# A GEGLU feed-forward kernel: sixteen start-up transposes in one run, and the first two token blocks loaded in halves

## The chip, the core and the metric

The kernel runs on one core of one Trainium2 chip. The time is device time in microseconds of one execution. Three executions took 300.17, 300.36 and 300.91 us, a median of 300.36. A fourth execution, which took 300.01 us, was profiled; its span from the first to the last instruction is 298.7 us.

## What is computed

```python
B, S, D, F = 32, 32, 1024, 3584          # x is (B, S, D), all bfloat16
def reference(x, w_gate, w_up, w_down):
    return (_gelu(x @ w_gate) * (x @ w_up)) @ w_down
```

With tokens flattened there are N = 1024 tokens, D = 1024 features and F = 3584 hidden features. GELU is the tanh approximation.

## The kernel before

It is written engine by engine: each of the five engines has a program (`prog_sp`, `prog_act`, `prog_pool`, `prog_pe`, `prog_dve`, L317 to L482) whose instructions run in the order written. Order between engines is kept by counting semaphores ("clocks"): `wait` stops an engine's program until a count is reached.

**The tiling.** F is cut into 28 chunks of 128 hidden features. A "part" (L140 to L149) is one chunk against one range of tokens, and gives a gate product (key G) and an up product (key U), each the sum of eight matmuls over the eight slices dk of D. ScalarE applies GELU to the gate sum (L442), VectorE multiplies by the up sum (L475) and writes the hidden activations `hT`. After all parts, TensorE multiplies `hT` with `w_down` in 17 jobs (L423).

**x must be transposed**, since a matmul wants D on the partitions. There are two ways of doing it here.

- The first 256 tokens (`XA`) are two blocks b of 128 tokens. Each is loaded with tokens on the partitions (`xa`, L295): block 0 by SP's queue, block 1 by ACT's. TensorE turns each of the 2 x 8 squares of 128 x 128 by a matmul against an identity (`turn_xa`, L349 to L359) into PSUM banks 3 to 7, as listed in `XA_PS` (L130): bank 3 takes dk 0, bank 4 dk 1, bank 5 dk 2 and 3, bank 6 dk 4 and 5, bank 7 dk 6 and 7. Each bank is then copied to `xT` (`xa_copy`, L302 to L307): bank 7 by ScalarE, where `ACT_EARLY` = 9 places the copy behind its ninth early load, the others by VectorE.
- The other 768 tokens (pieces `XB1`, `XB2`, `XC2`) are loaded by L285 and transposed by VectorE in squares of 32 (L466). `dve_order` (L50 to L58) mixes these with VectorE's products: `E` is a product, `A`, `B`, `C`, `D` are transposes of the pieces, the digit is the part or the dk.

**The start on TensorE** (`prog_pe`, L395): 14 matmuls on constants (`WARM`: six with 512 columns, eight with 128), then a wait for the identity and for both blocks of x, then the list `steps` (L36 to L47):

```python
steps += [("X", 0), ("X", 1), ("X", 2)]    # turn banks 3, 4, 5
together(range(0, 4), 0, 1)                # parts 0-3: G then U, dk 0
steps += [("X", 3), ("X", 4)]              # turn banks 6, 7
together(range(0, 4), 1, 2)                # parts 0-3, dk 1
together(range(4, 8), 0, 2)
together(range(0, 8), 2, 6)
```

As bank 5 holds dk 2 and 3, the first line has eight transposes and the fourth line the other eight. Parts 0 to 7 sum in banks 0 to 7, so part 3's first matmul also waits until bank 3 is copied out, part 4's until bank 4 is, and so on. Parts 8 to 15 are the same chunks against tokens 256 to 511, and parts 16 to 23 the same chunks against tokens 512 to 1023.

**The first weights** are pieces `W0` (L134): for dk 0 and 1 two pieces of 128 KB each (512 columns), then 256 KB pieces. SP issues those of `w_gate`, ACT those of `w_up` (`early_loads`, L294 to L300), after the block of x and ahead of the other pieces of x. Every matmul waits for its own piece (L370).

Of the kernel before, what the change touches and what calls it, by code (L numbers as in the profile page):

```python
# [5 lines left out]
P = 128  # L6
# [49 lines left out]
class _Ctx:  # L56
# [11 lines left out]
    def set(self, key, val):  # L68
        assert key not in self.cur, key
        if self.prev is not None and key in self.prev:  # L70
            assert self.prev[key] == val, (key, self.prev[key], val)
        elif self.emit:
            raise AssertionError(f"mark {key} unknown in emit pass")
        self.cur[key] = val
        return val
# [9 lines left out]
def bass_standalone__geglu_ffn__sampling_kernel(  # L85
# [13 lines left out]
    DK = D // P  # L99
# [29 lines left out]
    XPIECES = [XB1, XB2, XC2]  # L129
    XA_PS = [(3, 0, 1), (4, 1, 2), (5, 2, 4), (6, 4, 6), (7, 6, 8)]  # L130
    XA_ACT = (4,)
    ACT_EARLY = 9

    W0 = [(0, 1, 0, 512), (1, 2, 0, 512), (0, 1, 512, 1024), (1, 2, 512, 1024)]  # L134
    W0 += [(k, k + 1, 0, 1024) for k in range(2, 6)]
# [10 lines left out]
    for n, (m, h) in enumerate(rest):  # L146
        b = 2 * (n % 4)
# [13 lines left out]
    steps = []  # L161

    def together(ps_, k0, k1, tok=None):
        for dk in range(k0, k1):
            for key in ("G", "U"):
                for p in ps_:
                    steps.append((p, key, dk, tok))
# [4 lines left out]
                for dk in range(k0, DK):  # L172
                    steps.append((p, key, dk, None))

    steps += [("X", 0), ("X", 1), ("X", 2)]
    together(range(0, 4), 0, 1)
    steps += [("X", 3), ("X", 4)]
    together(range(0, 4), 1, 2)
    together(range(4, 8), 0, 2)
    together(range(0, 8), 2, 6)  # L180
    one_by_one(range(0, 8), 6)
# [26 lines left out]
    def evac_eng_is_act(ji):  # L208
        return ji % 2 == 0

    out_r = of.rearrange("(tc p) d -> p tc d", p=P)
    xa_r = xf.rearrange("(b p) d -> p b d", p=P)
# [5 lines left out]
    C_PE = _Clock("pe")  # L218
    C_ACT = _Clock("act")
    C_DVE = _Clock("dve")  # L220
    C_POOL = _Clock("pool")
    Q_XA = [_Clock(f"xa{b}", 16) for b in range(2)]
    Q_X = {(q, s): _Clock(f"x{i}{s}", 16) for i, q in enumerate(XPIECES) for s in range(2)}
    Q_W0 = {(w, p): _Clock(f"{w}0k{p[0]}c{p[2]}", 16) for p in W0 for w in ("wg", "wu")}
    Q_WG = [_Clock(f"wg{j}", 16) for j in range(NG)]
    Q_WU = [_Clock(f"wu{j}", 16) for j in range(NG)]
    Q_WD_SP = _Clock("wd_sp", 16)
    Q_WD_POOL = _Clock("wd_pool", 16)
    Q_OUT = _Clock("out", 16)
    all_clocks = [C_PE, C_ACT, C_DVE, C_POOL, *Q_XA, *Q_X.values(), *Q_W0.values(), *Q_WG, *Q_WU,  # L230
                  Q_WD_SP, Q_WD_POOL, Q_OUT]

    ctx = _Ctx()

    with ExitStack() as es:
        def sb(name, shape, dtype):
            return es.enter_context(nc.sbuf_tensor(name, shape, dtype))
# [6 lines left out]
        xa = hT[:, FM - 10:FM - 8, :]  # L244
        ident = sb("ident", [P, P], BF16)
# [8 lines left out]
        ps = es.enter_context(nc.psum_tensor("ps", [P, 8, 512], FP32))  # L254
# [27 lines left out]
        def load_x(ew, eng, q, side):  # L282
            c0, c1 = q[0] // 32, q[1] // 32
            for a in (2 * side, 2 * side + 1):
                v = ew.do(lambda: eng.dma_start(  # L285
                    xs[32 * a:32 * (a + 1), c0:c1, :], x_r[a, :, c0:c1, :]), clock=Q_X[(q, side)])
            ctx.set(("x", q, side), v)

        def load_w0(ew, eng, w, p):
            k0, k1, f0, f1 = p  # L290
            ctx.set((w + "0", p), ew.do(lambda: eng.dma_start(
                big[w][:, k0:k1, f0:f1], w_r[w][:, k0:k1, f0:f1]), clock=Q_W0[(w, p)]))

        def early_loads(ew, eng, side):  # L294
            yield ctx.set(("xa", side), ew.do(lambda: eng.dma_start(  # L295
                xa[:, side, :], xa_r[:, side, :]), clock=Q_XA[side]))
            for p in W0:
                yield load_w0(ew, eng, ("wg", "wu")[side], p)
            for q in XPIECES:
                yield load_x(ew, eng, q, side)  # L300
# [45 lines left out]
                    osb[:, tc, col0:col0 + ncols]), clock=Q_OUT)  # L346
            sp.wait(Q_OUT, last)

        def turn_xa(pe, eng, j):  # L349
            bank, k0, k1 = XA_PS[j]  # L350
            for dk in range(k0, k1):
                for b in range(2):
                    o = 256 * (dk - k0) + P * b
                    last = dk == k1 - 1 and b == 1
                    v = pe.do(lambda: eng.matmul(  # L355
                        ps[:, bank, o:o + P],
                        xa[:, b, :].rearrange("p (j k) -> p j k", k=DK)[:, :, dk],
                        ident[:, :], start=(dk == k0 and b == 0), stop=last), mark=last)
            ctx.set(("XP", j), v)  # L359

        def part_step(pe, eng, opened, i, key, dk, tok):
            m, t0, t1, gs, us = parts[i]
            w, (bank, f0, f1) = ("wg", gs) if key == "G" else ("wu", us)
            if tok is not None:
                f0, f1 = f0 + tok[0] - t0, f0 + tok[1] - t0
                t0, t1 = tok
            buf, slot, j = slot_of[m]
            if j is None:
                p = next(p for p in W0 if p[0] <= dk < p[1] and p[2] <= m * P < p[3])
                pe.wait(Q_W0[(w, p)], ctx.get((w + "0", p)))  # L370
            else:
                pe.wait((Q_WG if w == "wg" else Q_WU)[j], ctx.get((w, j)))
            if bank in bank_before[i]:
                pe.wait(C_DVE, ctx.get(("D", bank_before[i][bank])))
            for jx, (xbank, k0, k1) in enumerate(XA_PS):
                if t0 == XA[0] and (xbank == bank or k0 <= dk < k1):
                    pe.wait(C_ACT if jx in XA_ACT else C_DVE, ctx.get(("XA", jx)))
            for q in XPIECES:
                if q[0] < t1 and t0 < q[1]:
                    pe.wait(C_DVE, ctx.get(("T", dk, q)))  # L380
            first = (i, bank) not in opened
            opened.add((i, bank))
            last = (dk == DK - 1)
            v = pe.do(lambda: eng.matmul(  # L384
                ps[:, bank, f0:f1],
                wbuf(w, buf)[:, dk, slot * P:(slot + 1) * P],
                xT[:, dk, t0:t1],
                start=first, stop=last and (key == "U" or gs[0] != us[0]),
            ), mark=last)
            if last:  # L390
                ctx.set((key, i), v)

        WARM = [512] * 6 + [128] * 8

        def prog_pe(eng):  # L395
            pe = _Eng(ctx, eng, C_PE)
            for n in WARM:
                pe.do(lambda: eng.matmul(ps[:, 0, 0:n], ones_w, ones_x[:, 0:n],  # L398
                                         start=True, stop=True), mark=False)
            pe.wait(C_POOL, ctx.get("ident"))  # L400
            for b in range(2):
                pe.wait(Q_XA[b], ctx.get(("xa", b)))
            opened = set()
            for step in steps:
                if step[0] == "X":
                    turn_xa(pe, eng, step[1])
                else:
                    part_step(pe, eng, opened, *step)
            pe.wait(Q_WD_SP, ctx.get("wd_sp_total"))
            pe.wait(Q_WD_POOL, ctx.get("wd_pool_total"))  # L410
            bank_last_job = {}
            for ji, (tc, col0, ncols, b) in enumerate(jobs):
                if b in bank_last_job:
                    pj = bank_last_job[b]
                    pe.wait(C_ACT if evac_eng_is_act(pj) else C_DVE, ctx.get(("E", pj)))
                else:
                    pe.wait(C_DVE, ctx.get(("D", owner[b])))
                bank_last_job[b] = ji
                v = None
                for m in range(FM):  # L420
                    pe.wait(C_DVE, ctx.get(("D", last_part[m])))
                    last = (m == FM - 1)
                    v = pe.do(lambda: eng.matmul(  # L423
                        ps[:, b, 0:ncols],
                        hT[:, m, tc * P:(tc + 1) * P],
                        wd[:, m, col0:col0 + ncols],
                        start=(m == 0), stop=(m == FM - 1),
                    ), mark=last)
                ctx.set(("O", ji), v)

        def prog_act(eng):
            act = _Eng(ctx, eng, C_ACT)
            act.do(lambda: eng.activation(warm[:, 0:1], const0, ACTF.Gelu_apprx_tanh))  # L433
            for n, _ in enumerate(early_loads(act, eng, 1)):
                if n == ACT_EARLY - 1:
                    for j in XA_ACT:
# [14 lines left out]
        def prog_dve(eng):  # L451
# [34 lines left out]
            (prog_act, nc.scalar, "scalar"),  # L486
            (prog_pool, nc.gpsimd, "gpsimd"),
            (prog_pe, nc.tensor, "tensor"),
            (prog_dve, nc.vector, "vector"),
        ]  # L490
# [42 lines left out]
```

## Time and profile before

| what | value |
|---|---|
| median of three executions | 300.36 us (300.17 to 300.91) |
| the profiled execution: its time, its span | 300.01 us, 298.7 us |
| TensorE matmuls busy | 294.0 us, 98% of the span |
| VectorE, ScalarE busy | 58.4 us (20%), 42.0 us (14%) |
| bytes moved | 26.43 MB |
| share of the chain that ended last: TensorE | 97% |

The chain of waits follows the last instruction back to what released it. A busy TensorE says only that some matmul was in flight. Near the start a line of the timeline gives the start in microseconds, the length, the engine, the line, the operation and how many instructions are merged in it, and in brackets how long the engine had idled and what ended that. PEld is the loading of a matmul's stationary operand; a name with a q is an engine's queue, where a DMA is issued.

### The profile page before, as it was taken

What the parts mean: (1) busy time and instruction counts of PE and PEld (TensorE: products, weight loads), DVE (VectorE), ACT (ScalarE), POOL (GpSimd) and SP (SyncE); (2) the same over time, 40 slices, a digit from 0 to 9 for tenths busy, and PEclk for the clock granted to TensorE, in tenths of its full rate; (3) what the DMA queues carried; (4) which work ended last, traced back from release to release, by engine and by line L of the source; (5) the groups of instructions that cost most, each with busy time, mean ns of one, the idle gap of its engine ahead of it and who ended that gap; (6) DMA issues with size and microseconds to landing.
All of it is one profiled execution on the core that took longest, in us unless ns stands there. A gap on an engine that the chain in (4) does not pass through costs nothing.

```text
span 298.7 us, 3500 instructions
## 1 busy us (share of the span) xinstructions
PE 294.0 (98%) x1538; PEld 149.6 (50%) x1562; DVE 58.4 (20%) x96; ACT 42.0 (14%) x76; POOL 7.4 (2%) x13
## 2 busy tenths in 40 slices
PE   8999999999999999999999999999999999999997
PEld 5899644444444444444444444444444444444446
DVE  2069722111112111112111112210000000000000
ACT  2042211112111112111112111110000000000000
POOL 0001001020001002001000000000000000000000
DMA  7988003856008300942103000000000100010001
GB/s 247 380 217 267 19 1 116 306 174 250 0 0 281 142 0 21 372 171 83 59 0 140 0 2 0 0 2 18 18 18 20 35 18 18 20 35 18 18 20 35
DMA packets 18894, 26.43 MB, mean 88 GB/s; under 512 B 1088, under 2 KB 13504, under 8 KB 18880
## 3 DMA queue, kind: packets, MB, share of 16 engines
q1 hardware_dynamic: 13232, 14.68, 15.1%
q0 software_dynamic: 2176, 8.39, 7.9%
q10 hardware_dynamic: 3472, 3.15, 3.3%
q8 instruction: 12, 0.20, 0.3%
q14 instruction: 2, 0.02, 0.0%
HBM read 24.12 MB, written 2.10 MB: 88 GB/s over the span
## 4 chain that ended last, share of the span: by engine, by line
PE 97%; DMA 1%; issue 1%; ACT 0%; DVE 0%
PE ps L384 65%; PE ps L423 32%; DMA hT<-in_x_dram 1%; PE ps L355 0%; DVE xT L305 0%; ACT xT L448 0%; ACT L433 0%
## 5 line engine op out<-in xcount | busy, mean ns | idle before, releaser
L423 PE MATMUL ps<-wd,hT 128*128 128x512 bf16 (+1 forms) x468 | 96.5, 366 | 0.4
L384 PE MATMUL ps<-xT,wgbig 128*128 128x512 bf16 (+2 forms) x394 | 79.6, 336 | 0.6 <-DVE xT L305 0.2
L384 PE MATMUL ps<-xT,wubig 128*128 128x512 bf16 (+2 forms) x395 | 79.8, 336 | 0.3
L423 PEld LDWEIGHTS ps<-wd,hT 128*128 128x128 bf16 x476 | 46.6, 98 | 50.4
L475 DVE TENSOR_TENSOR hT<-tb,ps 128x512 bf16<-128x512 f32 (+1 forms) x64 | 39.2, 615 | 142.4 <-PE ps L384 142.3
L442 ACT ACTIVATE tb<-ps 128x512 f32<-128x512 f32 (+1 forms) x64 | 34.8, 544 | 156.6 <-PE ps L384 156.0
L384 PEld LDWEIGHTS ps<-xT,wgbig 128*128 128x128 bf16 x400 | 38.0, 98 | 31.9 <-DVE xT L466 0.5
L384 PEld LDWEIGHTS ps<-xT,wubig 128*128 128x128 bf16 x400 | 38.1, 98 | 31.4
L384 PE MATMUL ps<-xT,wgsmall 128*128 128x512 bf16 x126 | 30.1, 379 | 0.1
L384 PE MATMUL ps<-xT,wusmall 128*128 128x512 bf16 x125 | 29.8, 379 | 0.2
L481 DVE CAST xT<-ps 128x512 bf16<-128x512 f32 (+1 forms) x8 | 5.3, 659 | 88.1 <-PE ps L423 88.1
L384 PEld LDWEIGHTS ps<-xT,wgsmall 128*128 128x128 bf16 x128 | 12.5, 98 | 15.1
L384 PEld LDWEIGHTS ps<-xT,wusmall 128*128 128x128 bf16 x128 | 12.5, 98 | 15.1
L448 ACT ACTIVATE xT<-ps 128x512 bf16<-128x512 f32 (+1 forms) x9 | 5.2, 573 | 93.1 <-PE ps L423 93.1
L466 DVE STREAM_TRANSPOSE xT<-hT 128x128 bf16<-128x128 bf16 (+2 forms) x20 | 13.3, 701 | 0.0
L279 POOL DMA_DIRECT2D wubig<-in_w_up_dram x3 | 2.7, 884 | 64.0 <-PE ps L384 64.0
L398 PE MATMUL ps<-const-bfloat16-1.0 128*128 128x128 bf16 (+1 forms) x14 | 3.3, 408 | 0.8 <-PEq L518 0.8
L279 POOL DMA_DIRECT2D wusmall<-in_w_up_dram x2 | 1.9, 973 | 47.7 <-PE ps L384 26.0
L305 DVE CAST xT<-ps 128x256 bf16<-128x256 f32 (+1 forms) x4 | 2.0, 553 | 5.3 <-PE ps L355 5.3
L273 POOL DMA_DIRECT2D wd<-in_w_down_dram x3 | 2.3, 764 | 19.1 <-PE ps L384 19.1
L398 PEld LDWEIGHTS ps<-const-bfloat16-1.0 128*128 128x128 bf16 x14 | 1.5, 128 | 2.5 <-issue 2.5
L355 PE MATMUL ps<-ident,hT 128*128 128x128 bf16 x16 | 1.3, 226 | 0.3 <-DMA hT<-in_x_dram 0.3
(9 smaller groups left out, 4.0 us busy)
## 6 DMA issues: line engine op xcount, KB each, us to landing
wd<-in_w_down_dram SPq DMA_DIRECT2D x4, 1024.0 KB, 11.5
wgbig<-in_w_gate_dram SPq DMA_DIRECT2D x3, 1024.0 KB, 5.7
wubig<-in_w_up_dram POOLq DMA_DIRECT2D x3, 1024.0 KB, 9.6
wd<-in_w_down_dram POOLq DMA_DIRECT2D x3, 1024.0 KB, 11.1
wgsmall<-in_w_gate_dram SPq DMA_DIRECT2D x2, 1024.0 KB, 7.0
wusmall<-in_w_up_dram POOLq DMA_DIRECT2D x2, 1024.0 KB, 9.6
out_dram<-xT SPq DMA_DIRECT2D x15, 128.0 KB, 1.7
wgbig<-in_w_gate_dram SPq DMA_DIRECT2D x6, 256.0 KB, 7.4
```

The source lines that it names most:

```text
L273: ew.do(lambda: eng.dma_start(wd[:, a:b, :], wd_r[:, a:b, :]), clock=clock)
L279: ctx.set((w, j), ew.do(lambda: eng.dma_start(wbuf(w, buf)[:, :, 0:gsz * P], w_r[w][:, :, c0 * P:(c0 + gsz) * P]), clock=q))
L305: ctx.set(("XA", j), ew.do(lambda: copy(xT[:, k0:k1, XA[0]:XA[1]], ps[:, bank, 0:256 * (k1 - k0)].rearrange("p (k t) -> p k t", t=256))))
L355: v = pe.do(lambda: eng.matmul(ps[:, bank, o:o + P], xa[:, b, :].rearrange("p (j k) -> p j k", k=DK)[:, :, dk], ident[:, :], start=(dk == ...
L384: v = pe.do(lambda: eng.matmul(ps[:, bank, f0:f1], wbuf(w, buf)[:, dk, slot * P:(slot + 1) * P], xT[:, dk, t0:t1], start=first, stop=last ...
L398: pe.do(lambda: eng.matmul(ps[:, 0, 0:n], ones_w, ones_x[:, 0:n], start=True, stop=True), mark=False)
L423: v = pe.do(lambda: eng.matmul(ps[:, b, 0:ncols], hT[:, m, tc * P:(tc + 1) * P], wd[:, m, col0:col0 + ncols], start=(m == 0), stop=(m == F ...
L442: ctx.set(("A", i), act.do(lambda: eng.activation(t_bufs[i % NTB][:, 0:t1 - t0], ps[:, gb, g0:g1], ACTF.Gelu_apprx_tanh)))
L448: ctx.set(("E", ji), act.do(lambda: eng.activation(osb[:, tc, col0:col0 + ncols], ps[:, b, 0:ncols], ACTF.Copy)))
L466: v = dve.do(lambda: eng.transpose(xT[:, dk, q[0]:q[1]].rearrange("p (c i) -> p c i", i=32), src))
L475: ctx.set(("D", i), dve.do(lambda: eng.tensor_tensor(hT[:, m, t0:t1], t_bufs[i % NTB][:, 0:t1 - t0], ps[:, ub, u0:u1], ALU.mult)))
L481: ctx.set(("E", ji), dve.do(lambda: eng.tensor_copy(osb[:, tc, col0:col0 + ncols], ps[:, b, 0:ncols])))
```

## The change

All sixteen transposes are put ahead of the first useful matmul, in the order: block 0 dk 0 to 3, block 1 dk 0 to 3, block 0 dk 4 to 7, block 1 dk 4 to 7. A step is now one transpose, and waits for the two halves of its own block only. Each block is loaded as two transfers of 64 tokens (64 partitions, 128 KB): tokens 0 to 63 of each block by SP, 64 to 127 by ACT. The eight constant matmuls with 128 columns are gone, and `ACT_EARLY` is 10, as ScalarE's queue has one more early load.

```diff
-    ACT_EARLY = 9
+    ACT_EARLY = 10
...
-    steps += [("X", 0), ("X", 1), ("X", 2)]
-    together(range(0, 4), 0, 1)
-    steps += [("X", 3), ("X", 4)]
-    together(range(0, 4), 1, 2)
+    for k0 in (0, 4):
+        for b in range(2):
+            steps += [("X", b, dk) for dk in range(k0, k0 + 4)]
+    together(range(0, 4), 0, 2)
...
-    Q_XA = [_Clock(f"xa{b}", 16) for b in range(2)]
+    Q_XA = {(b, e): _Clock(f"xa{b}{e}", 16) for b in range(2) for e in range(2)}
...
         def early_loads(ew, eng, side):
-            yield ctx.set(("xa", side), ew.do(lambda: eng.dma_start(
-                xa[:, side, :], xa_r[:, side, :]), clock=Q_XA[side]))
+            r = slice(64 * side, 64 * side + 64)
+            for b in range(2):
+                yield ctx.set(("xa", b, side), ew.do(lambda: eng.dma_start(
+                    xa[r, b, :], xa_r[r, b, :]), clock=Q_XA[(b, side)]))
...
-        def turn_xa(pe, eng, j):
+        def turn_xa(pe, eng, b, dk):
+            for e in range(2):
+                pe.wait(Q_XA[(b, e)], ctx.get(("xa", b, e)))
+            j = next(j for j, (_, k0, k1) in enumerate(XA_PS) if k0 <= dk < k1)
             bank, k0, k1 = XA_PS[j]
...
+            o = 256 * (dk - k0) + P * b
+            last = dk == k1 - 1 and b == 1
+            v = pe.do(lambda: eng.matmul(
+                ps[:, bank, o:o + P],
+                xa[:, b, :].rearrange("p (j k) -> p j k", k=DK)[:, :, dk],
+                ident[:, :], start=(dk == k0 and b == 0), stop=last), mark=last)
+            if last:
+                ctx.set(("XP", j), v)
...
-        WARM = [512] * 6 + [128] * 8
+        WARM = [512] * 6
...
-            for b in range(2):
-                pe.wait(Q_XA[b], ctx.get(("xa", b)))
             opened = set()
             for step in steps:
                 if step[0] == "X":
-                    turn_xa(pe, eng, step[1])
+                    turn_xa(pe, eng, *step[1:])
```

## The prediction

> **What bounds the kernel now.** I read the page's head first, then the chain of waits over the first 30 us, then the timelines of the engines around the start, last who waits for VectorE. The head and its fourth part:
>
> ```profile
> span 298.7 us, 3500 instructions
> ...
> PE 294.0 (98%) x1538; PEld 149.6 (50%) x1562; DVE 58.4 (20%) x96; ACT 42.0 (14%) x76; POOL 7.4 (2%) x13
> ...
> PE 97%; DMA 1%; issue 1%; ACT 0%; DVE 0%
> ```
>
> TensorE is the bound nearly from end to end. The change adds and removes no useful matmul, so it can only move the point from which TensorE runs without pause. That point lies in the first microseconds, which the chain shows (start, length, what):
>
> ```profile
> 0.86 3.39 DMA hT<-in_x_dram
> 4.25 0.14 issue
> 4.38 0.33 PE ps L355 x2
> 4.71 0.02 issue
> 4.73 0.43 DVE xT L305
> 5.17 0.14 issue
> 5.30 1.03 PE ps L384 x8
> 6.34 0.49 PE ps L355 x8
> ```
>
> Block 1 of x, issued at 0.86, lands at 4.25. Two transposes, VectorE's copy of bank 3 and a hand-over later, the first useful matmul starts at 5.30. After eight of them the other eight transposes cut in for 0.49. TensorE's timeline gives the starts exactly:
>
> ```profile
> 5.30 0.60 PE L384 MATMUL ps<-xT,wgbig 128*128 128x256 bf16 x4 [0.24 <-DVE xT L305]
> ...
> 6.17 0.65 PE L355 MATMUL ps<-ident,hT 128*128 128x128 bf16 x8
> 6.66 0.60 PE L384 MATMUL ps<-xT,wgbig 128*128 128x256 bf16 x4
> ```
>
> Its weight loads (PEld) show the pace of the constant matmuls, which wait for nothing:
>
> ```profile
> 2.93 0.15 PEld L398 LDWEIGHTS ps<-const-bfloat16-1.0 128*128 128x128 bf16 x1 [0.28 <-issue]
> 3.35 0.57 PEld L398 LDWEIGHTS ps<-const-bfloat16-1.0 128*128 128x128 bf16 x7 [0.28 <-issue]
> ```
>
> There is a second narrow place. From 26.14 VectorE works without a pause to the last transpose of x, and TensorE's next weight load waits for that one (VectorE's timeline, then PEld's):
>
> ```profile
> 26.14 0.42 DVE L475 TENSOR_TENSOR hT<-tb,ps 128x256 bf16<-128x256 f32 x1 [0.36 <-PE ps L384]
> ...
> 34.36 1.08 DVE L466 STREAM_TRANSPOSE xT<-hT 128x512 bf16<-128x512 bf16 x1
> ```
>
> ```profile
> 35.49 0.10 PEld L384 LDWEIGHTS ps<-xT,wgbig 128*128 128x128 bf16 x1 [0.50 <-DVE xT L466]
> ```
>
> So TensorE restarts at 35.49 at VectorE's word. A gain at the start survives only if VectorE's run moves with it.
>
> **The change part by part.** Times are those of the profiled execution, 300.01 us: its span of 298.7 and 1.3 around it.
>
> *Transposes moved.* Eight take 0.49, so 0.061 each. Before, from block 1's landing to the first matmul of dk 1 is 6.66 - 4.25 = 2.41 us: 0.13 hand-over, 0.92 from 4.38 to 5.30, eight matmuls 0.87 (5.30 to 6.17), eight transposes 0.49. After, the first four transposes need block 0 alone. SP's transfer lands 2.9 us after its issue at 0.80, at 3.7, so four of 0.061 are done before 4.25 and cost nothing; if block 0 came only with block 1, they would cost 0.24. From 4.25: 0.13 hand-over; block 1's dk 0 is the very next transpose and ends 0.23 later (a transpose's median length), at 4.61; VectorE starts 0.03 later, copies 0.43, and with 0.14 hand-over the first useful matmul can start at 5.21. The twelve transposes still queued end at 4.38 + 12 x 0.061 = 5.11, so they hide behind that copy. The eight matmuls take 0.87, and dk 1 starts at 6.08 instead of 6.66: a gain of 0.58.
>
> *Copies.* VectorE's four run 4.64 to 5.07, 5.50, 6.1 and 6.8 (their lengths before are 0.41 to 0.69). First uses: bank 4's copy by dk 1 at 6.08, banks 5 and 6 by parts 5 and 6 near 7. Cost nothing. ScalarE's copy of bank 7 waits for the last transpose, 5.3 instead of 6.8, so the two weight pieces and six x pieces queued behind it on ACT are issued up to 1 us earlier. ACT is one issue later with its first ten loads.
>
> *Loads in halves.* Each queue issues one load more, 0.38 to 0.43 long, and ten weight pieces and six x pieces on each are issued that much later (behind the x pieces on SP, and behind a wait for them on POOL, stand only the loads of parts 24 on, issued at 22.4 and 22.9 and used from 61.6). What hides it: transfers stand in line. The up piece of dk 2 is issued at 3.22 and lands 6.2 later, at 9.42, while early pieces took 3.7; the line, not the issue, sets the landing, and the bytes are the same. Bounds for block 1's landing, from the table of stretches: all that moved from 1.8 to 3.9, where the 0.52 MB of both blocks lie, went at 312 GB/s; the x pieces that are also written to a part of the partitions moved at 243 GB/s (14.6 to 21.8), the best weight stretch at 391 (8 to 13). That is 2.16 or 1.34 us against 1.68: 0.48 later to 0.34 earlier. I take 0, being nearest to the first row, which is this same transfer. Weights: 0 to 0.43 later; I take 0.1, as the line is long.
>
> The Trainium skill, "DMA: Bandwidth & Descriptors" (Rules for kernel authors), speaks against this edit: transfers to disjoint partition halves share the same sixteen engines and serialize, so it advises one full transfer. The trace leans that way: two whole blocks issued 0.06 apart landed at 3.7 and 4.25, one after the other. "SBUF — State Buffer" (Door 1) adds that 64 partitions reach only half of the DMA ports; by it alone the blocks would take up to twice 1.68, and the gain of 0.58 would turn into an estimated loss of 1.1, unless both queues' halves are in flight together, as they should be here.
>
> *Weights as the cap.* Each piece's landing against its use before: gate dk 0 4.6 and 5.27; up dk 1 6.0 and 6.99; up dk 2 9.42 and 10.05; gate dk 3 9.8 and 10.92. The tightest has 0.63, less some 0.06 hand-over: the gain can't pass 0.57, and with weights 0.1 later, 0.47.
>
> *Constant matmuls removed.* Eight of them end at 4.10, before x is there: no direct gain. Their cover is the clock: the 512-column ones come 0.43 apart (2.93 to 3.35), while useful 512-column matmuls later come 0.216 apart. So TensorE starts at half pace and reaches full pace about 3.6, inside the eight, after 2.75 us of work. I take 0, as six matmuls still reach 3.56; the price if not is rival 2.
>
> *At 35.49.* VectorE's run starts from products that TensorE releases (17.32, 26.14), so it moves by the same 0.47, if XB1 is there: its last transfer lands at 18.3, the first transpose of it starts at 18.97 now and would at 18.5. It passes, with 0.2 spare.
>
> Sum: 0.58 from the order, cut to 0.47 by weights: 300.01 becomes 299.5. The median of the runs lies 0.35 above the profiled execution, so for a median: 300.36 - 0.47 = **299.9**.
>
> **The rivals.** *1, the gain is lost on the way.* If each weight piece lands 0.43 later, the cap is 0.14; if x also lands 0.48 later, the sum is -0.3; or XB1 comes 0.7 later and VectorE hands the old time back at 35.49. For it: the 0.63 and 0.2 are all there is. Against: unchanged bytes. Time 300.2 to 300.7.
>
> *2, the clock opens late (slower).* Place: TensorE idles from 3.56 until block 0 lands, with 2.7 us of work behind it, just short of what opened the clock before. At half pace a transpose takes 0.107 (0.427/4), twelve end at 5.67, the first matmul starts 0.48 later than forecast, and matmuls lose 0.49 us per us until the opening. After 2.75 us counted from 4.39 that is 7.1: 1.2 lost in all, 301.1. Counted from the useful matmuls, 8.45: 1.8 lost, 301.7. It decides (0.9 above the median) from an opening at 7.5. Against: before, idle gaps of 0.43 and 0.35 between weight loads at 4.35 and 5.27 cost no pace. The granted clock reads 1.00 in every stretch, so only spacings tell.
>
> The Trainium skill, "TensorE: Matmul & The Clock Gate" (Part 1), gives about 3.4 us of sustained work in a free-running window; this trace opened after 2.75. By the page alone an estimated opening is 4.25 at the earliest, and six matmuls don't fill a window; the next end of a window is then at an estimated 7.7, which by the same losses gives 301.4 instead of 299.9.
>
> *3, more than forecast.* The halves arrive in better order, x 0.34 earlier and the weights with it: gain 0.9, 299.4 or less. Against: the cap of the weights.
>
> **How the numbers follow.** About 0.3%, 0.9 us, is what a measurement of this kernel can tell from no change (299.46 to 301.26). Forecast 0.48, its own range 299.4 to 300.3, with 0.06 of it below 299.46; rival 1 0.16, of which 0.02 slower, where both delays add up with a late XB1; rival 2 0.25, of which 0.17 beyond 301.26; rival 3 0.11, below. Faster 0.17, same 0.64, slower 0.19. The range goes from 299.1 (most of rival 3) to 301.5 (half of rival 2's spread).
>
> **What would show it.** Right: first L384 matmul near 5.2, the first of dk 1 near 6.1 with no transpose between, no wait over 0.1 for a weight piece, TensorE after VectorE's last transpose near 35.0. Order wrong: the copy of bank 3 starts after 4.8. Loads wrong: block 1 later than 4.5, or the up piece of dk 2 after 9.6. Clock wrong: L384 matmuls of 256 columns 0.213 apart instead of 0.109 after 5.2. The prediction falls if TensorE's restart at 35.49 doesn't move, or moves by over 1 us.

## The result, and the profile after

The changed kernel takes 302.16 us, a median of six executions (302.09 to 303.73), against 300.19 for six of the kernel before that ran beside it (299.92 to 300.91). The ratio is 1.0073, with a 95% interval of 1.0058 to 1.0088: slower by 0.7%, where the forecast was 299.9. The profiled execution took 302.13 us; its page begins:

```profile
span 300.9 us, 3511 instructions
...
PE 296.6 (99%) x1554; PEld 150.0 (50%) x1554; DVE 58.3 (19%) x96; ACT 42.0 (14%) x76; POOL 7.3 (2%) x13
...
PE 97%; DMA 1%; ACT 0%; issue 0%
```

TensorE is still the bound, with the same useful matmuls; the span is 2.2 us longer. The chain of waits over the first 40 us (start, length, what) shows where it sets out:

```profile
1.44 4.00 DMA hT<-in_x_dram
5.44 0.14 issue
5.57 1.48 PE ps L358 x12
7.05 30.57 PE ps L388 x295
```

Block 1 of x is there at 5.44 instead of 4.25, although its transfer is no larger and its last half is issued only 0.58 later. Then come the twelve transposes, and TensorE runs on without a wait until VectorE's last transpose. TensorE's timeline shows a second thing:

```profile
3.97 0.62 PE L358 MATMUL ps<-ident,hT 128*128 128x128 bf16 x4 [0.41 <-DMA hT<-in_x_dram]
5.57 1.48 PE L358 MATMUL ps<-ident,hT 128*128 128x128 bf16 x12 [0.98 <-DMA hT<-in_x_dram]
6.84 1.06 PE L388 MATMUL ps<-xT,wgbig 128*128 128x256 bf16 x4
...
8.55 0.85 PE L388 MATMUL ps<-xT,wgbig 128*128 128x256 bf16 x4
9.23 0.60 PE L388 MATMUL ps<-xT,wubig 128*128 128x256 bf16 x4
```

Four matmuls of 256 columns take 1.06 at first and 0.60 from 9.23 on. The transposes are 0.107 apart, not 0.061. So the clock was at half pace from the start until about 9.1; before, it was at full pace from 3.6. The first matmul of dk 1 is at 8.55 instead of 6.66, 1.89 later. Of that, 1.19 is x. Behind x, the half pace makes the path longer than the forecast's by 1.28 (0.44 up to the first useful matmul, at 6.84, and 0.84 in the eight that follow), and the order takes off the 0.58 that was forecast for it. Four more slow matmuls add 0.24, which makes 2.13. The wait at VectorE's word, at 35.49 before, has moved by as much, 2.14:

```profile
37.63 0.10 PEld L388 LDWEIGHTS ps<-xT,wgbig 128*128 128x128 bf16 x1 [0.50 <-DVE xT L468]
```

The queue that issues the loads has changed too. SP's timeline before, then after:

```profile
0.80 0.38 SPq L295 DMA_DIRECT2D hT<-in_x_dram  x1
1.24 5.22 SPq L291 DMA_DIRECT2D wgbig<-in_w_gate_dram  x10
```

```profile
0.80 1.20 SPq L297 DMA_DIRECT2D hT<-in_x_dram  x2
2.05 5.92 SPq L291 DMA_DIRECT2D wgbig<-in_w_gate_dram  x10
```

One issue of 128 KB to 64 partitions takes longer than one of 256 KB to 128 partitions, and the first weight piece is issued at 2.05, not 1.24. Each transfer leaves sixteen completion counts in the trace, and the kernel waits for all sixteen: block 1's last one is at 5.44, and the transposes go on at 5.57. The first and the last count, for the up piece of dk 2 and its neighbours, tell how far the parts of a transfer are apart (us):

```
                       before: issued  first  last     after: issued  first  last
block 1 (later half)          0.86     3.74   4.25            1.44    4.40   5.44
up piece of dk 2              3.22     8.52   9.42            4.39    8.66  10.99
gate piece of dk 3            3.60     9.21   9.78            4.57    9.60  11.36
up piece of dk 3              3.70     9.87  10.79            4.88   10.57  12.36
```

The first parts land less than a microsecond later than before; the last ones land 1.2 to 1.6 later, and a matmul waits for the last. So there are two suspects: the *loads* in halves, which make x and the weights late, and the *clock*, which opened late once eight constant matmuls were gone.

### The profile page after: what moved, and what is told of

Read it like the earlier page. It is cut to its first block, busy times and chain, and to the rows that moved or that the text cites. A ratio compares the mean times of both kernels' runs of the same rounds, so it can differ in the third digit from the quotient of the medians.

```text
span 300.9 us, 3511 instructions
## 1 busy us (share of the span) xinstructions
PE 296.6 (99%) x1554; PEld 150.0 (50%) x1554; DVE 58.3 (19%) x96; ACT 42.0 (14%) x76; POOL 7.3 (2%) x13
## 4 chain that ended last, share of the span: by engine, by line
PE 97%; DMA 1%; ACT 0%; issue 0%
PE ps L388 65%; PE ps L425 32%; DMA hT<-in_x_dram 1%; PE ps L358 0%; ACT L435 0%; ACT xT L450 0%
## 5 line engine op out<-in xcount | busy, mean ns | idle before, releaser
L388 PE MATMUL ps<-xT,wgbig 128*128 128x512 bf16 (+2 forms) x400 | 80.9, 339 | 0.0
L402 PE MATMUL ps<-const-bfloat16-1.0 128*128 128x512 bf16 x6 | 2.7, 624 | 0.8 <-PEq L520 0.8
L358 PE MATMUL ps<-ident,hT 128*128 128x128 bf16 x16 | 2.1, 310 | 1.4 <-DMA hT<-in_x_dram 1.4
L358 PEld LDWEIGHTS ps<-ident,hT 128*128 128x128 bf16 x16 | 1.7, 163 | 2.5 <-issue 1.3
## 6 DMA issues: line engine op xcount, KB each, us to landing
wd<-in_w_down_dram POOLq DMA_DIRECT2D x3, 1024.0 KB, 11.1
```

The costliest lines, as they stand in the source:

```text
L358: v = pe.do(lambda: eng.matmul(ps[:, bank, o:o + P], xa[:, b, :].rearrange("p (j k) -> p j k", k=DK)[:, :, dk], ident[:, :], start=(dk == ...
L388: v = pe.do(lambda: eng.matmul(ps[:, bank, f0:f1], wbuf(w, buf)[:, dk, slot * P:(slot + 1) * P], xT[:, dk, t0:t1], start=first, stop=last ...
```

## The experiments

Each kernel ran beside the kernel before, on the same chip. Times are medians of ten executions unless another number is given, ratios are to that kernel before. What a trace shows is one execution, whose own time can lie well off the median.

### Undoing the parts one at a time

**e1**, the eight constant matmuls put back into the changed kernel:

```diff
-        WARM = [512] * 6
+        WARM = [512] * 6 + [128] * 8
```

> The changed kernel with its eight 128-column constant matmuls put back. Clock theory (without them TensorE's clock doesn't open at 3.6, and runs at half pace to 9.1): it opens near 3.6 again, block 1 still lands near 5.4, the first useful matmul starts near 6.4 and the first of dk 1 near 7.3, some 0.6 later than before the change: 300.8. Load theory (the halves' late landing is all that costs, the eight are idle work): as the changed kernel, 302.1.

Measured: 302.3 us (301.44 to 302.8, four executions), ratio 1.007 (1.0049 to 1.0091). In the profiled execution (301.88) the clock theory's trace came true, and its time did not. TensorE is at full pace from the twelve transposes on:

```profile
6.04 0.93 PE L358 MATMUL ps<-ident,hT 128*128 128x128 bf16 x12 [1.20 <-DMA hT<-in_x_dram]
...
7.77 0.60 PE L388 MATMUL ps<-xT,wgbig 128*128 128x256 bf16 x4
```

Block 1 landed at 5.90 here, and still the first matmul of dk 1 came at 7.77 instead of 8.55. But then TensorE waited for weights, as its list of waits says (total us, times, longest):

```profile
PEld ps L388 <- DMA wubig<-in_w_up_dram: 0.9, 2, 0.6
...
PEld ps L388 <- DMA wgbig<-in_w_gate_dram: 0.2, 1, 0.2
```

It reached VectorE's word at 37.38, only 0.25 before the change does. So with an open clock the late weights cost nearly as much in this execution as the slow clock does in the change's.

**e2**, the changed kernel with whole loads, and six constant matmuls still:

```diff
-            r = slice(64 * side, 64 * side + 64)
-            for b in range(2):
-                yield ctx.set(("xa", b, side), ew.do(lambda: eng.dma_start(
-                    xa[r, b, :], xa_r[r, b, :]), clock=Q_XA[(b, side)]))
+            yield ctx.set(("xa", side), ew.do(lambda: eng.dma_start(
+                xa[:, side, :], xa_r[:, side, :]), clock=Q_XA[side]))
...
-            for e in range(2):
-                pe.wait(Q_XA[(b, e)], ctx.get(("xa", b, e)))
+            pe.wait(Q_XA[b], ctx.get(("xa", b)))
```

> The changed kernel with each block loaded as one transfer of 128 tokens again, block 0 by SP and block 1 by ACT; still six constant matmuls. Load theory: block 1 lands at 4.25, the gap behind the constant matmuls is short, the clock opens near 3.6 to 4.5, and the forecast's 299.7 comes out. Clock theory: block 1 lands at 4.25, but the clock stays at half pace until some 3.5 after 4.4, near 7.9: 301.2 to 301.5.

Measured: 299.88 us (299.5 to 300.25), ratio 0.9986 (0.9977 to 0.9996). The load theory's number, and nearly the forecast's. Block 1 landed at 4.25 again. Yet in the profiled execution the clock was late here as well:

```profile
3.98 1.90 PE L355 MATMUL ps<-ident,hT 128*128 128x128 bf16 x16 [0.42 <-DMA hT<-in_x_dram]
5.68 1.01 PE L385 MATMUL ps<-xT,wgbig 128*128 128x256 bf16 x4
6.52 0.60 PE L385 MATMUL ps<-xT,wubig 128*128 128x256 bf16 x4
```

Sixteen transposes at half pace, full pace only from about 6.5, and yet that execution took 300.25, the slowest of the ten and no slower than the median of the kernel before, 300.28.

**e3**, the order alone: e2 with all fourteen constant matmuls.

> Only the new order of transposes: whole loads and all fourteen constant matmuls, as before the change. Both theories: the forecast's sum, 0.47 below the kernel before, 299.7; the first matmul of dk 1 near 6.1 and TensorE after VectorE's last transpose near 35.0. If the order itself costs: 300.2 or more.

Measured: 300.03 us (299.42 to 301.31), ratio 0.9987 (0.9964 to 1.0009). Its first matmul of dk 1 is at 5.92, 0.74 ahead of the kernel before, of which 0.14 is block 1's earlier landing (4.11). But at VectorE's word, at 35.35, it is only 0.14 ahead. The other 0.60 was handed back where the last two weight pieces (dk 6 and 7, columns 512 on) came late, at 17.48 and 18.04; what made them late was not tested. Its weight loads:

```profile
17.52 0.11 PEld L385 LDWEIGHTS ps<-xT,wgbig 128*128 128x128 bf16 x2 [0.36 <-DMA wgbig<-in_w_gate_dram]
18.08 0.11 PEld L385 LDWEIGHTS ps<-xT,wubig 128*128 128x128 bf16 x2 [0.44 <-DMA wubig<-in_w_up_dram]
```

**e4**, the kernel before with six constant matmuls.

> The kernel before with only the six 512-column constant matmuls. Clock theory: the useful matmuls from 5.35 on run at half pace until 7 to 8, 0.8 to 1.5 lost: 301.0 to 301.7. Load theory: no difference, 300.2.

Measured: 300.13 us, ratio 1.0011 (0.9989 to 1.0033). As the load theory said; the profiled execution's eight transposes take 0.69 from 4.44, full pace. Four of its ten executions took 300.8 to 302.2, though, more spread than e2 and e3 show. None of those four was profiled, so whether the clock was late in them stays open.

**e5**, the kernel before with nothing changed but the halves: the load lines of the change, and a wait for all four.

> The kernel before (its order, its fourteen constant matmuls) with nothing changed but the two blocks loaded as halves of 64 tokens. If the halves alone carry the loss: block 1 lands between 5.2 and 6, the up piece of dk 2 near 11 instead of 9.4, 301.5 to 302.5. If halves cost only together with the new order: 300.2.

Measured: 302.74 us (302.26 to 303.33, four executions), ratio 1.0085 (1.0068 to 1.0101). The halves alone cost 2.5 us. With e1 and e2 this settles the change's loss: every kernel so far with the halves loses about two microseconds or more, whatever its order and constant matmuls, and none of the three without them loses. The loss takes another shape here than in e1: in the profiled execution TensorE waited for no weight piece, but block 1 landed at 5.95 and the clock fell back to half pace from 7.7 to 11.1, with all fourteen constant matmuls ahead of it.

### What about the halves is slow

The next kernels start from e1: the new order and fourteen constant matmuls.

**e6**, two transfers a block, of half of the features to all 128 partitions:

```diff
-            r = slice(64 * side, 64 * side + 64)
+            r = slice(512 * side, 512 * side + 512)
...
-                    xa[r, b, :], xa_r[r, b, :]), clock=Q_XA[(b, side)]))
+                    xa[:, b, r], xa_r[:, b, r]), clock=Q_XA[(b, side)]))
```

> The changed kernel with fourteen constant matmuls, each block still as two transfers of 128 KB, one a queue, but all 128 tokens by half of the features (1 KB rows). Partition theory (a transfer to 64 partitions is what is slow): block 1 lands near 4.3 to 4.6, the up piece of dk 2 near 9.5, 300.0 to 300.3. Count theory (one transfer more on each queue is what costs): as with token halves, block 1 after 5.2, 301.5 or more.

Measured: 300.75 us (300.15 to 302.92), ratio 1.0023 (1.0005 to 1.0041). Most of the loss is gone: block 1 landed at 4.31, issues took 0.38 to 0.46. But 0.5 against the kernel before is left, and the up piece of dk 2 landed at 9.81, later than the 9.5 of the partition theory.

**e7**, halves of 64 tokens, each queue with a block of its own:

```diff
-            for b in range(2):
+            b = side
+            for e in range(2):
+                r = slice(64 * e, 64 * e + 64)
```

> The changed kernel with fourteen constant matmuls, halves of 64 tokens, but block 0 as both of its halves on SP and block 1 as both on ACT, so that the two queues begin with the same partitions. Partition theory with shared ports: as slow as the change or slower, 302 to 303. Theory that splitting one block over two queues is the trouble: 300.3.

Measured: 301.99 us (301.31 to 302.47, four executions), ratio 1.0057 (1.0038 to 1.0076). As slow as the change, so it isn't splitting one block over two queues. Block 1 landed at 6.22, later than the change's 5.44, but the time is no longer; whether two queues hinder each other on the same partitions stays open.

**e8**, one transfer of 256 KB a queue, 64 tokens of both blocks (`xa[r, 0:2, :]`):

> The changed kernel with fourteen constant matmuls, where SP loads tokens 0 to 63 of both blocks in one transfer of 256 KB and ACT tokens 64 to 127; all transposes wait for both. Partition theory: both land after 5, the up piece of dk 2 near 10.5 to 11, 301.5 to 302.5. Count theory: both land near 4.3, 300.2.

Measured: 301.16 us (300.76 to 302.88), ratio 1.0039 (1.0022 to 1.0057). With no more transfers than before, the two land at 4.42 and 5.45, 1.03 apart, where whole blocks of the same size landed 0.54 apart. So 64 partitions cost time without any further transfer. Six of the executions took 300.8 to 301.3 and four 302.2 to 302.9. The profiled one, 302.88, is of the slower four. In it TensorE waited for no weight piece; the clock was at half pace until 10.1, although all fourteen constant matmuls were there:

```profile
5.59 1.90 PE L357 MATMUL ps<-ident,hT 128*128 128x128 bf16 x16 [1.17 <-DMA hT<-in_x_dram]
...
8.99 1.06 PE L387 MATMUL ps<-xT,wgbig 128*128 128x256 bf16 x4
```

**e9**, **e10** and **e11** take the even tokens on SP and the odd ones on ACT, so that a transfer writes 64 partitions that aren't neighbours: in e1, in the changed kernel itself, and in e8.

```diff
-            r = slice(64 * side, 64 * side + 64)
+            r = slice(side, P, 2)
```

> As the change with fourteen constant matmuls, still two transfers of 64 tokens a block, but SP takes the even tokens and ACT the odd ones, so that each transfer writes 64 partitions spread over all 128. Neighbour theory (64 neighbouring partitions share too few ways in): block 1 lands near 4.3 to 4.6, the up piece of dk 2 near 9.5 to 9.9, 300.2 to 300.9. Number theory (64 partitions, whichever, are slow to issue and to write): block 1 after 5.2, 301.5 to 302.5.

> The changed kernel itself, six constant matmuls, with even and odd tokens in place of lower and upper halves. Neighbour theory: block 1 near 4.4 and a clock that opens late but behind weights that set the pace, 299.9 to 300.9. Number theory: 302.1 as the change.

> One transfer a queue for both blocks (as the run with one half each), but SP takes even tokens and ACT odd ones. Neighbour theory: the two land 0.5 apart instead of 1.03, the later one near 4.4, 300.0 to 300.6. Number theory: 5.4 and 301.2 as with lower and upper halves.

Measured: e9 302.05 us (300.72 to 302.92), ratio 1.0041 (1.0016 to 1.0066); e10 301.97, 1.0049 (1.0021 to 1.0076); e11 302.3, 1.0046 (1.0021 to 1.0072). Executions spread over two to three microseconds, so the three can't be ranked among themselves, but no median comes near 300.3. The neighbour theory falls for the time. About x it was right in e9 alone, where block 1 landed at 4.61; in e10 it landed at 5.12, and in e11 the two transfers landed at 4.05 and 5.13, about as far apart as e8's. Nor did the early x help in e9 (profiled: 302.52), for the weights behind were late, which its list of waits shows:

```profile
PE ps L388 <- DMA wgbig<-in_w_gate_dram: 1.7, 2, 0.9
```

So an x that lands early is not enough for a repair; the whole line of loads is late.

How the halves' loss comes about differs between the profiled executions. In e1, e6 and e9 TensorE waited for weight pieces. In the change, e5, e7, e8, e10 and e11 it waited for none: x was late, and the clock was at half pace until 8.6 to 11.1. Four of these six (e5, e7, e8 and e11) have all fourteen constant matmuls. So putting the eight back does not by itself keep the clock open, and what decides between the two courses is not shown; what all of them have in common is the cut-up loads.

**e13 to e16** measure the transfers by themselves: the kernel before, with 2.1 MB of x read ahead of everything else. e13's lines are shown; the others differ in the slice, and e16 loads four whole blocks a queue.

```diff
         def early_loads(ew, eng, side):
+            r = slice(64 * side, 64 * side + 64)
+            for c in range(8):
+                v = ew.do(lambda: eng.dma_start(hT[r, c, :], xa_r[r, c, :]), clock=Q_D[side])
+            ctx.set(("dum", side), v)
...
+            for s in range(2):
+                dve.wait(Q_D[s], ctx.get(("dum", s)))
             for what in dve_order:
```

> The kernel before, with 2.1 MB of x read ahead of everything else (into space used only later; VectorE's first product waits for it), as eight transfers of 128 KB on each queue, tokens 0 to 63 of each block by SP, 64 to 127 by ACT. Both slow theories: 230 to 290 GB/s, issues 0.55 or longer, the last one landed near 10 to 11. If 64 partitions cost only at the start: 340 to 390 GB/s, landed near 8. The time as a whole is some 5 to 9 over the kernel before and tells nothing more.

> The same 2.1 MB, even tokens by SP and odd ones by ACT. Number theory: as lower and upper halves, near 10 to 11. Neighbour theory: 340 to 390 GB/s, landed near 8.

> The same 2.1 MB in as many transfers, each to all 128 partitions with 1 KB rows. If 64 partitions are the trouble: issues 0.38 to 0.45, 330 to 390 GB/s, landed near 8. If the number of transfers is: near 10.

> The same 2.1 MB as four whole blocks on each queue, 2 KB rows on 128 partitions. All theories: issues 0.38 to 0.45, 350 to 400 GB/s, landed between 7 and 8.

The whole times, 307.8 to 310.5 in one execution each, tell nothing more, as the added reads hold up everything behind them. Below is the table of stretches, 3 to 7 us, in which nothing but these transfers moved; the last two columns are the busy share of the DMA engines and GB/s. For e13, e14, e15 and e16:

```profile
3.00:7.00 4.00, 1.18 (x10) 0.72 (x8) 0.00 (x0) 0.00 (x0) 0.00 (x0) 1.00 0.94 262
```

```profile
3.00:7.00 4.00, 1.42 (x10) 0.88 (x8) 0.00 (x0) 0.00 (x0) 0.00 (x0) 1.00 0.97 273
```

```profile
3.00:7.00 4.00, 1.42 (x10) 0.87 (x8) 0.00 (x0) 0.00 (x0) 0.00 (x0) 1.00 0.96 289
```

```profile
3.00:7.00 4.00, 1.42 (x10) 0.87 (x8) 0.00 (x0) 0.00 (x0) 0.00 (x0) 1.00 1.05 394
```

| | rows and partitions | one issue on SP, median | GB/s, 3 to 7 | last one landed |
|---|---|---|---|---|
| e13 lower and upper | 2 KB, 64 | 0.60 | 262 | 11.70 |
| e14 even and odd | 2 KB, 64 | 0.60 | 273 | 11.02 |
| e15 feature halves | 1 KB, 128 | 0.43 | 289 | 10.27 |
| e16 whole blocks | 2 KB, 128 | 0.42 | 394 | 8.70 |

Neither simple theory of the expectations, partitions alone or number of transfers alone, gives all four; e16, too, landed later than the 7 to 8 expected. Sixteen transfers instead of eight, each half as large, cost 1.57 (e16 to e15), a cost that e6 paid in small. Sending them to 64 partitions costs 0.75 to 1.43 more (e15 to e14 and e13), and 0.17 per issue. Which 64 partitions matters less, 0.68. Row size changes too between e15 and the other three and wasn't told apart, and each of the four was profiled once.

The DMA engines were busy 0.94 to 1.05 of the time in all four, so it isn't the longer issue that holds these transfers back. The trace's packet records show where the time goes: packets of 2 KB that started in this stretch took 84 ns at the median in e13, e14 and e16 alike, but 115, 114 and 86 ns on average. The slowest twentieth took over 250 ns in e13 and e14, and over 87 in e16. So between these three a few long packets make most of the difference; why 64 partitions bring them stays open.

### The version that is left

**e12** is e2 again, in more rounds.

> The changed kernel with whole loads again, in more rounds, to tell its gain from none: the forecast's step for the order alone gave 0.47; the first runs gave 0.4 under the kernel before. Expected 299.8 to 299.9, a ratio of 0.9985 to 0.999.

Measured: 299.79 us (299.53 to 301.17, twelve executions) against 300.41, ratio 0.9978 (0.9956 to 1.0). With e2's 299.88 against 300.28, the new order with whole loads is some 0.4 to 0.6 us faster than the kernel before, at the edge of what can be told, and 2.3 faster than the change. Of the kernels with the new order and whole loads, only e3's trace shows the gain: the profiled executions of e2 and e12 (300.25 and 300.37) are slower than their medians and come to VectorE's word at 35.78 and 35.89, behind the 35.49 of the kernel before.

## Why the prediction was wrong

The step that failed is *Loads in halves*, in its sentence "the line, not the issue, sets the landing, and the bytes are the same". The same bytes did not take the same time. The step's two terms were 0 for x and 0.1 for the weights; measured were 1.19 (5.44 against 4.25) and, at the up piece of dk 2, 1.57 (10.99 against 9.42). A second term at 0, for the constant matmuls, failed with it: in the change's profiled execution the half pace cost 1.28 and 0.24. Only the loads decide the time, though: with whole loads and the same six constant matmuls the loss is gone (e2). The bounds failed too. The upper one, 0.48, came from an average over x pieces of 32 partitions and 512-byte rows, which shared their stretch with weights, and an average rate doesn't tell when the last of a transfer's sixteen parts lands. And the issue's length was taken from a transfer to 128 partitions; that of the new shape was 0.54 to 0.84.

Point by point:

- *Transposes moved*: right. e3's first matmul of dk 1 came at 5.92 with block 1 at 4.11; 0.60 is the order's, for a forecast of 0.58. In e3 no transpose or copy held up a useful matmul after the first.
- *Weights as the cap*: of the right size as far as can be told, wrong in place. e3 and e12 gained some 0.25 and 0.6, for 0.47, and e3's interval does not exclude that there is no gain; in e3 the gain was cut not at dk 2 but at the last weight pieces, 17.5 to 18.1, which the step didn't look at.
- *Constant matmuls removed*, taken as 0: the time agrees (e1 302.3 and the change 302.16; e4 ratio 1.0011), the reasoning doesn't, so that is luck. "Six matmuls still reach 3.56" did not open the clock in the changed kernel, nor did fourteen in e8; and where it was open, in e1, late weights cost as much.
- *At 35.49*: right that VectorE's run and TensorE's restart move together, here by 2.14 and later. The 0.2 to spare for XB1 were not there: in e3 it landed at 18.83 instead of 18.3, and VectorE waited 0.6 for it, but had caught up by 25.99, where it waited for TensorE again.
- *Rival 1* named what happened, x and weights later together, and priced it at a third: 0.43 and 0.48 where 1.57 and 1.19 came. Its 300.2 to 300.7 should have reached past 302, on the slower side.
- *Rival 2* had the right sign, and the clock did open later than its 7.5. But it doesn't explain the loss by itself: in e1's profiled execution the clock was open in time and the kernel as slow, and in e2's it opened at 6.5 and the loss was gone.

The Trainium skill's advice in "DMA: Bandwidth & Descriptors" (Rules for kernel authors), not to split a transfer into disjoint partition halves, was right, and the prediction set it aside. It speaks of transfers that serialize; here they were also slower, 262 against 394 GB/s, part of which (289) goes with the smaller transfers of e15. The estimate by "SBUF — State Buffer" (Door 1), a loss of 1.1 us, had the right sign. Its reason, that 64 partitions reach only half of the ports, explains little here: by the same section's mapping the even partitions reach all sixteen, and they moved at 273 GB/s.

## What to carry to other kernels

A transfer that is cut up is a new shape, and its price is read from a transfer of that shape or bounded far more widely than by an average rate: look at the issue's length, at the last of its parts to land, and at everything queued behind it. Where a start-up stage is fed by one line of loads, a microsecond lost by its first transfers comes back in the later ones (here 1.6 at the pieces of dk 2 and 3), and speeding up the consumer, by order or by clock, gains only what the line has to spare. When two causes show in a trace, undo each alone: here putting back the constant matmuls, as the more visible one, the clock, suggested, gained nothing, and whole loads gained everything.

## What the runs showed of the hardware

- Issuing 128 KB to 64 partitions took 0.54 to 0.84 us (e13, e14 and the change), 256 KB to 128 partitions 0.38 to 0.45 (before and e16, the blocks of x at the start). In the change the weight piece right behind, to 128 partitions, took 0.58 on SP and 0.60 on ACT too, against 0.42 and 0.46 before.
- The clock's opening moves about. Full pace came at 3.6 (before), before 4.4 (e4, six constant matmuls), about 6.5 (e2) and about 9.1 (the change); with fourteen constant matmuls and the halves, at about 8.6 (e7) and 10.1 (e8). In e5, after 1.7 us without a matmul, eight transposes ran at full pace from 6.09, and those at 8.04 at half pace again.
- The granted clock in the table of stretches reads 1.00 for the change from 6.8 to 9.0, at half pace, and 0.50 for e13 from 8 to 10, when TensorE has been idle since 4.2. So it does not show a clock that has yet to open for the first time.
